# Combination by neighbouring tokens with 1 MB stores, and the softmax exponent a step later, in a long convolution with a soft mixture of experts

## Chip, cores, metric

One core of one Trainium2 chip. Times are device microseconds (us) of that core. In the profiles PE is the engine that runs this kernel's matrix products (PEld its weight loads), ACT its functions such as the exponent, DVE and POOL (GpSimd) its vector work, and SP issues nearly all of its DMA transfers. SBUF is where the kernel's tiles lie (those of PE's products apart), on up to 128 partitions; HBM is what the transfers read and write at the other end (146.18 MB read and 128.52 MB written in the profile of before); PE's products are written to tiles named `bank`, `ap` or `op`, from which ACT or DVE "evict" them to SBUF (0.58 us for one of 128x512 on ACT, L251 of before). The kernel before: median 1210.75 us of 3 runs (1209.6 to 1213.64).

## The reference, cut to what matters

```python
# 8 batches of 5696 tokens of 128 channels, all float32
y = irfft(rfft(x, n=2*S) * rfft(h, n=2*S))[:, :S]     # long convolution
x = y.reshape(45568, 128)
logits = x @ phi                                      # 32 slots: 8 experts of 4
d = softmax(logits, over tokens);  slot_input = d.T @ x
slot_out = relu(slot_input @ w1[e]) @ w2[e]           # per expert, hidden size 1024
c = softmax(logits, over slots)
return c @ slot_out                                   # 45568 x 128, 23.33 MB
```

`d` needs all tokens before the experts can start, so the combination `c @ slot_out` and all stores of the output come at the very end. `c` is kept transposed until then, that of the early chunks in HBM and at the end all of it in SBUF (`cT`).

## The kernel before

The convolution is done by two levels of small transforms. One loop of 95 steps runs everything in a pipeline: `stage_a` and `stage_b1/b2` ("units", up to three a step) are the transforms, `stage_c1` makes a chunk's `y`, and the stages after it the logits and both softmaxes. Every second step a new window of two chunks gets a common maximum: `window_top` and `window_row` make it (`mr`), GpSimd subtracts it (`d`), ACT takes the exponent. I call these window steps, the others plain steps. A chunk `c` is at `stage_c1` in step `c + 26`.

```python
    def stage_c3(c):                       # logits, then the softmax over slots
        ...
        nc.gpsimd.tensor_tensor(out=ct[...], in0=L[...], in1=rm..., op=AL.subtract)   # L329
        nc.scalar.activation(ct[:, :, :], ct[:, :, :], AF.Exp)                        # L332
        cs[c] = ct

    def stage_c3b(c):                      # row sums on DVE (L338-L340), product on GpSimd (L341)
    def stage_c4(c):                       # transpose c on PE (L349), evict on ACT

    # ... one step of the loop (cut)
        slot_b()                           # a unit: stage_b1(u), then stage_b2(u - 1)
        if c1 is not None: stage_c2(c1)
        if new: window_top(r // WC)
        if c is not None: stage_c1(c)
        if new: window_row(r // WC)        # mr, d = L - mr on GpSimd, exp(d) on ACT
        slot_b()
        if c1 is not None: stage_c3(c1)
        if t < NA: stage_a(t, 1); fold(t + 1, 1)
        slot_b()
        if c1 is not None: stage_c3b(c1)
        if chunk(2) is not None: stage_c4(chunk(2))

    # the end: 14 groups of rows r, all batches in one product
    sizes = [1] + [8] * 9 + [4] * 4
    for size in sizes:
        ...                                # 4 products per row, evictions on ACT and DVE
        for b in range(B):                 # a batch is 16 partitions
            k = 2 * NJ * b
            nc.sync.dma_start(out=ov[b, :, r0:r0 + size, :],
                              in_=o_[k:k + 2 * NJ, 0:size, :, :].rearrange("p r q d -> p r (q d)"))
```

What matters for the order: in the timelines of this case, DVE and ACT run their instructions in the order of this program, and one that waits holds up those behind it. In the kernel before, ACT starts L332 at 1057.71 after a wait of 2.10 us, and L354 behind it, whose product (L349) ended at 1055.55, follows only at 1058.03. DVE starts L338 at 1058.16 after a wait of 1.27 us, and L399 behind it, whose product (L397) ended at 1057.09, follows only at 1058.93.

## Time and profile before

| part of the span (from the trace) | us |
|---|---|
| start, to the first `stage_c1` product (L290, chunk 0) | 195.7 |
| loop, chunks 0 to 46 | 673.2 |
| late steps, chunks 46 to 55 (no `stage_a` any more) | 103.8 |
| drain, chunks 55 to 63 (no units any more) | 68.1 |
| last chain, chunk 63 to the last update of `acc` | 23.4 |
| experts, to the copy that makes `so4` | 15.6 |
| combination and stores, to the end | 129.9 |

The parts are cut at starts of instructions in one profiled run, so they sum to its span of 1209.6 us.

### The profile page before, as it was taken

The page shows a single profiled execution, that of the slowest core. Times are in us where ns is not written, and L with a number is a line of the kernel's source. Part 1 is how long each engine was busy: PE and PEld are TensorE (multiplying, and loading weights), DVE is VectorE, ACT ScalarE, POOL GpSimd, SP SyncE. Part 2 cuts the span into 40 slices and gives each one's busy share as a digit, 9 for nine tenths or more (in the row PEclk, how much of TensorE's full clock was granted, in tenths as well). Part 3 has the DMA queues.
Part 4 walks back from the last instruction along what each step waited for, and adds up shares of the span by engine and source line. Part 5 has one row for each costly group of instructions (what it writes and reads, how often), then busy time and mean ns, then how long its engine had stood idle before and what let it go on. Part 6 is the DMA issues. An engine that isn't in the chain of part 4 may idle for free.

```text
span 1209.6 us, 19085 instructions
## 1 busy us (share of the span) xinstructions
PE 1068.5 (88%) x6295; PEld 714.1 (59%) x6295; DVE 669.5 (55%) x1574; ACT 491.8 (41%) x1109; POOL 316.0 (26%) x352
## 2 busy tenths in 40 slices
PE   7788999999999999999999999999999989774430
PEld 3345665666666666666666666666667655453430
DVE  3144665666666666656665666666677745442210
ACT  4475444444444444444444444444433325421210
POOL 6433222233222322232222222222111114300000
PEclk9899999999999999999999999999999988877555
DMA  8999999887887788788788887887677766608888
GB/s 229 286 298 295 325 289 301 241 248 220 248 236 222 221 234 234 220 246 234 222 228 245 233 234 214 246 241 223 193 235 236 220 182 183 188 15 194 188 193 186
DMA packets 181576, 275.98 MB, mean 228 GB/s; under 512 B 14712, under 2 KB 121208, under 8 KB 175719
## 3 DMA queue, kind: packets, MB, share of 16 engines
q1 hardware_dynamic: 180903, 274.31, 79.5%
q8 instruction: 52, 0.85, 0.3%
q10 hardware_dynamic: 576, 0.46, 0.2%
q14 instruction: 45, 0.37, 0.1%
HBM read 146.18 MB, written 128.52 MB: 227 GB/s over the span
## 4 chain that ended last, share of the span: by engine, by line
PE 72%; SPq 10%; DVE 6%; DMA 5%; ACT 2%; issue 2%; POOL 2%; POOLq 0%; DVEq 0%; ACTq 0%
PE bank L182 18%; PE bank L290 17%; PE bank L248 12%; PE bank L212 12%; SPq L673 9%; PE bank L315 5%; PE bank L307 3%; DMA gt<-f 3%; PE ap L442 2%; DMA f<-fst 1%; POOL d L425 1%; DVE y L296 1%; DVE y L297 1%; DVE cm L322 1%; DVE pr L230 1%
## 5 line engine op out<-in xcount | busy, mean ns | idle before, releaser
L182 PE MATMUL bank<-x,s 128*128 128x512 f32 x576 | 279.4, 613 | 7.1 <-POOL x L171 7.1
L290 PE MATMUL bank<-zc,i 128*128 128x512 f32 x512 | 237.1, 607 | 5.3 <-DMA zc<-z 5.3
L212 PE MATMUL bank<-gt,wt 128*128 128x256 f32 x810 | 214.0, 387 | 17.0 <-DMA gt<-f 16.4
L171 POOL TENSOR_TENSOR x<-xc 89x512 f32<-89x512 f32 x144 | 182.9, 1271 | 134.9 <-PE bank L182 109.9
L212 PEld LDWEIGHTS bank<-gt,wt 128*128 128x128 f32 x810 | 151.0, 191 | 103.8 <-issue 75.9
L230 DVE TENSOR_TENSOR pr<-bank,Hr 128x512 f32<-128x512 f32 (+1 forms) x184 | 123.8, 673 | 132.4 <-PE bank L212 132.4
L248 PE MATMUL bank<-yf,vt 128*128 128x256 f32 x720 | 186.8, 381 | 9.9 <-DVE yf L236 5.0
L184 ACT ACTIVATE fst<-bank 90x512 f32<-90x512 f32 x288 | 162.1, 588 | 66.2 <-PE bank L182 54.5
L251 ACT ACTIVATE zst<-bank 128x512 f32<-128x512 f32 (+1 forms) x184 | 107.0, 582 | 178.4 <-PE bank L248 162.1
L182 PEld LDWEIGHTS bank<-x,s 128*128 128x128 f32 x576 | 102.6, 193 | 99.0 <-issue 61.9
L248 PEld LDWEIGHTS bank<-yf,vt 128*128 128x128 f32 x720 | 135.3, 190 | 36.3 <-ACT zst L251 6.5
L290 PEld LDWEIGHTS bank<-zc,i 128*128 128x128 f32 x512 | 94.3, 194 | 100.2 <-issue 96.6
L296 DVE TENSOR_TENSOR y<-bank,yo 89x512 f32<-89x512 f32 x64 | 44.0, 687 | 149.7 <-PE bank L290 82.3
L329 POOL TENSOR_TENSOR ct<-L,rm 89x256 f32<-89x256 f32 x64 | 39.2, 613 | 333.8 <-DVE rm L327 226.4
L230 DVE TENSOR_TENSOR pi<-bank,Hi 128x512 f32<-128x512 f32 (+1 forms) x184 | 122.7, 667 | 0.0
L315 PEld LDWEIGHTS bank<-phi,yt 128*89 128x89 f32 x1024 | 91.5, 160 | 15.9 <-ACT yt L308 10.9
L315 PE MATMUL bank<-phi,yt 128*89 128x32 f32 x1024 | 90.0, 242 | 8.1 <-ACT yt L308 8.1
L662 PE MATMUL op<-so,cT 32*128 32x128 f32 x712 | 43.5, 377 | 57.2 <-ACT o L670 56.8
L425 POOL TENSOR_TENSOR d<-L,mr 89x256 f32<-89x256 f32 x64 | 45.3, 727 | 167.7 <-DVE mr L417 167.7
L234 DVE TENSOR_TENSOR yf<-pr,pi 128x256 f32<-128x256 f32 (+1 forms) x184 | 80.3, 436 | 6.4
L332 ACT ACTIVATE ct<-ct 89x256 f32<-89x256 f32 x64 | 26.7, 417 | 122.7 <-POOL ct L329 122.7
L662 PEld LDWEIGHTS op<-so,cT 32*128 32x128 f32 x712 | 40.4, 272 | 60.2 <-ACT o L670 59.2
(78 smaller groups left out, 906.4 us busy)
## 6 DMA issues: line engine op xcount, KB each, us to landing
f<-fst SPq DMA_DIRECT2D x144, 360.0 KB
gt<-f SPq DMA_DIRECT2D x198, 256.0 KB
zc<-z SPq DMA_DIRECT2D x64, 720.0 KB
z<-zst SPq DMA_DIRECT2D x176, 256.0 KB
xc<-in_x_dram SPq DMA_DIRECT2D x64, 320.0 KB
out_dram<-o SPq DMA_DIRECT2D x72, 256.0 KB
c_t<-cst SPq DMA_DIRECT2D x54, 89.0 KB
cl<-c_t SPq DMA_DIRECT2D x6, 712.0 KB
```

Source lines behind the costliest of these rows:

```text
L171: nc.gpsimd.tensor_tensor(out=y_[0:R1, :, :], in0=t_[:, 0, :, :], in1=t_[:, 1, ::-1, :], op=AL.subtract if comp else AL.add)
L182: nc.tensor.matmul(p[:, :], s1[:, tab[G], :], src[:, :, :].rearrange("p n d -> p (n d)"), start=True, stop=True)
L184: nc.scalar.activation(st[:, :, G, :], p[0:N1, :].rearrange("p (n d) -> p n d", d=D), AF.Copy)
L212: nc.tensor.matmul(p[:, q * 256:(q + 1) * 256], wt[:, 2 * i + q, :], t_[:, q, :, :].rearrange("p c d -> p (c d)"), start=True, stop=True)
L230: nc.vector.tensor_tensor(out=t[:, 0:n, :, :], in0=pv[:, 0:n, :, :], in1=H[:, 2 * i:2 * i + n, :].unsqueeze(2).broadcast_to([P, n, 2, D]), ...
L234: nc.vector.tensor_tensor(out=y_[:, 0:n, 0, :], in0=pr[:, 0:n, 0, :], in1=pi[:, 0:n, 1, :], op=AL.subtract)
L248: nc.tensor.matmul(p[:, q * 256:(q + 1) * 256], vt[:, 2 * i + q, :], y_[:, q, :, :].rearrange("p c d -> p (c d)"), start=True, stop=True)
L251: nc.scalar.activation(st[:, 0:n, :], p[:, 0:n * 256].rearrange("p (q c) -> p q c", q=n), AF.Copy)
L290: nc.tensor.matmul(p[:, :], i1[:, tabs[q], :], t_[:, o, :, q, :], start=(q == 0), stop=(q == 1))
L315: nc.tensor.matmul(p[0:R1, i * NSL:(i + 1) * NSL], yt[:, i, :], phi[:, :], start=True, stop=True)
L662: nc.tensor.matmul(pq[q][:, k * D:(k + 1) * D], cT[rows, r0 + i + k, :], so4[rows, :], start=True, stop=True)
L673: nc.sync.dma_start(out=ov[b, :, r0:r0 + size, :], in_=o_[k:k + 2 * NJ, 0:size, :, :].rearrange("p r q d -> p r (q d)"))
```

## The change

The intent: stores of 1 MB from all 128 partitions, an exponent that ACT need not wait for, and w2 in longer runs. Core of the diff:

```diff
@@ the exponent leaves stage_c3 and comes a step later, after the window's row
-        nc.scalar.activation(ct[:, :, :], ct[:, :, :], AF.Exp)
         cs[c] = ct
+    def stage_c3x(c):
+        nc.scalar.activation(cs[c][:, :, :], cs[c][:, :, :], AF.Exp)
...
         if new:
             window_row(r // WC)
+        c2 = chunk(2)
+        if c2 is not None:
+            stage_c3x(c2)
+            stage_c3b(c2)
         slot_b()
...
-        if c1 is not None:
-            stage_c3b(c1)
-        if chunk(2) is not None:
-            stage_c4(chunk(2))
+        if chunk(3) is not None:
+            stage_c4(chunk(3))
@@ placement of c from HBM into cT: the mirrored half from ACT to GpSimd; 3 buffers, not 2
-        nc.scalar.activation(cT[:, :, e_ - n:e_], st[...], AF.Copy)
+        nc.gpsimd.tensor_copy(out=cT[:, b, :, e_ - n:e_], in_=st[...])
@@ combination: 8 rows of one batch per product, 4 products per store
-    ov = out.rearrange("(b r j n) d -> b j r (n d)", b=B, r=R1, n=CH)
+    ov = out.rearrange("(b t) d -> b t d", b=B)
...
+            nc.sync.dma_start(
+                out=ov[b, t0:t0 + n * RW * N2, :].rearrange("(w p n) d -> p w (n d)", p=P, n=CH),
+                in_=o_[:, 0:n, :, :].rearrange("p w q d -> p w (q d)"))
@@ w2
-                in_=moe_w2[2 * i:2 * i + 2].rearrange("e (c p) d -> p e c d", p=P))
+                in_=moe_w2[2 * i:2 * i + 2].rearrange("e (p c) d -> p e c d", p=P))
```

Cut: the hidden layer is evicted in the order that the new w2 wants; `cT` is indexed batch first; the one row left over goes out in a last store of 256 KB; `ct` has three buffers, `c4`, `dg` one, `ones` is narrower; the output tile is half as large and has five buffers, not three.

More of the change, by code (lines that the diff above doesn't have):

```diff
@@ L113 @@
     make_identity(nc, ident)
-    ones = const.tile([P, P], F32, name="ones")
+    ones = const.tile([P, R1], F32, name="ones")
     nc.gpsimd.memset(ones[:, :], 1.0)
@@ L124 @@
     ypool = work.enter_context(tc.tile_pool(name="ypool", bufs=1))
-    mid, inner = ExitStack(), ExitStack()
+    mid, inner, cload = ExitStack(), ExitStack(), ExitStack()
     ps = mid.enter_context(tc.tile_pool(name="ps", bufs=6, space=PSUM))
@@ L327, in stage_c3 @@
         nc.vector.reduce_max(out=rm[:, :], in_=L[:, :, :], axis=AX.X)
-        ct = cpool.tile([R1, 2 * CH, NSL], F32, name="ct", tag="ct")
+        ct = cpool.tile([R1, 2 * CH, NSL], F32, name="ct", tag="ct", bufs=3)
         nc.gpsimd.tensor_tensor(out=ct[:, :, :], in0=L[:, :, :],
@@ L364, in place @@
         b, j = divmod(c, NJ)
-        return tail["cT"][:, :, 2 * NJ * b + (2 * NJ - 1 - j if f else j)]
+        return tail["cT"][:, b, :, 2 * NJ - 1 - j if f else j]
     def load_c(c0, n):
@@ L374, in place_all @@
         b, j = divmod(c0, NJ)
-        k = 2 * NJ * b
+        e_ = 2 * NJ - j
         cT = tail["cT"]
-        nc.gpsimd.tensor_copy(out=cT[:, :, k + j:k + j + n],
+        nc.gpsimd.tensor_copy(out=cT[:, b, :, j:j + n],
                               in_=st[:, 0:n, 0, :].rearrange("p j r -> p r j"))
-        e_ = k + 2 * NJ - j
-        nc.scalar.activation(cT[:, :, e_ - n:e_],
-                             st[:, n - 1::-1, 1, :].rearrange("p j r -> p r j"), AF.Copy)
+        nc.gpsimd.tensor_copy(out=cT[:, b, :, e_ - n:e_],
+                              in_=st[:, n - 1::-1, 1, :].rearrange("p j r -> p r j"))
     mrows, downs, scales = {}, {}, {}
@@ L387, in window_max @@
         cm = cms[w % 2]
-        c4 = cpool.tile([R1, Q, NSL], F32, name="c4", tag="c4")
+        c4 = cpool.tile([R1, Q, NSL], F32, name="c4", tag="c4", bufs=1)
         nc.vector.tensor_tensor(out=c4[:, :, :],
@@ L406, in window_top @@
             downs[w] = df
-        dg = cpool.tile([P, NSL], F32, name="dg", tag="dg")
+        dg = cpool.tile([P, NSL], F32, name="dg", tag="dg", bufs=1)
         nc.vector.tensor_scalar(out=dg[:, :], in0=ident[:, 0:NSL], scalar1=top[:, w:w + 1],
@@ L414, in window_row @@
         p = bank()
-        nc.tensor.matmul(p[0:R1, 0:NSL], ones[:, 0:R1], dg[:, :], start=True, stop=True)
+        nc.tensor.matmul(p[0:R1, 0:NSL], ones[:, :], dg[:, :], start=True, stop=True)
         mr = cpool.tile([R1, NSL], F32, name="mr", tag="mr")
@@ L555 @@
             last = work.enter_context(tc.tile_pool(name="last", bufs=1))
-            tail["cT"] = last.tile([P, R1, B * 2 * NJ], F32, name="cT")
-            tail["pool"] = inner.enter_context(tc.tile_pool(name="cload", bufs=2))
+            tail["cT"] = last.tile([P, B, R1, 2 * NJ], F32, name="cT")
+            tail["pool"] = cload.enter_context(tc.tile_pool(name="cload", bufs=3))
             w2s = last.tile([P, E, NFC, D], F32, name="w2s")
@@ L576 @@
                 out=w2s[:, 2 * i:2 * i + 2, :, :],
-                in_=moe_w2[2 * i:2 * i + 2].rearrange("e (c p) d -> p e c d", p=P))
+                in_=moe_w2[2 * i:2 * i + 2].rearrange("e (p c) d -> p e c d", p=P))
     assert not (ys or Ls or ds or cs or prods or gs or zs or xs or folded or wait_b2
                 or kept or landed)
+    cload.close()
     rep4 = last.tile([P, Q, NSL], F32, name="rep4")
@@ L606 @@
     big = inner.enter_context(tc.tile_pool(name="big", bufs=2))
-    hid = big.tile([P, EG, F], F32, name="hid", tag="big")
+    hid = big.tile([P, EG, NFC, P], F32, name="hid", tag="big")
     hidT = big.tile([P, EG, NFC, P], F32, name="hidT", tag="big")
@@ L614 @@
                                  w1s[:, g * Q + q, f0:f0 + FH], start=True, stop=True)
+            dst = hid[:, g, :, f0 // NFC:(f0 + FH) // NFC]
+            src = p[:, :].rearrange("p (c k) -> p k c", k=NFC)
             if f0:
-                nc.vector.tensor_scalar(out=hid[:, g, f0:f0 + FH], in0=p[:, :], scalar1=0.0,
-                                        scalar2=None, op0=AL.max)
+                nc.vector.tensor_scalar(out=dst, in0=src, scalar1=0.0, scalar2=None, op0=AL.max)
             else:
-                nc.scalar.activation(hid[:, g, f0:f0 + FH], p[:, :], AF.Relu)
+                nc.scalar.activation(dst, src, AF.Relu)
     for g in range(EG):
@@ L624 @@
                 nc.tensor.transpose(p[:, k * P:(k + 1) * P],
-                                    hid[:, g, (k0 + k) * P:(k0 + k + 1) * P], ident[:, :])
+                                    hid[:, g, k0 + k, :], ident[:, :])
             (nc.vector.tensor_copy if k0 else nc.scalar.copy)(
@@ L646 @@
     cT = tail["cT"]
+    cL = last.tile([P, B, 2 * NJ], F32, name="cL")
+    nc.gpsimd.tensor_copy(out=cL[:, :, :], in_=cT[:, :, R1 - 1, :])
     ops = work.enter_context(tc.tile_pool(name="ops", bufs=8, space=PSUM))
-    opool = work.enter_context(tc.tile_pool(name="opool", bufs=3))
-    ov = out.rearrange("(b r j n) d -> b j r (n d)", b=B, r=R1, n=CH)
-    RG, G4 = 8, 4
-    sizes = [1] + [RG] * 9 + [G4] * 4
-    assert sum(sizes) == R1
-    r0 = 0
-    for size in sizes:
-        o_ = opool.tile([P, RG, Q, D], F32, name="o", tag="o")
-        for i in range(0, size, G4):
-            n = min(G4, size - i)
+    opool = work.enter_context(tc.tile_pool(name="opool", bufs=5))
+    ov = out.rearrange("(b t) d -> b t d", b=B)
+    RW = P // (2 * NJ)
+    NV = R1 // RW
+    assert NV * RW == R1 - 1
+    G4 = 4
+    for b in range(B):
+        for w0 in range(0, NV, G4):
+            n = min(G4, NV - w0)
+            lone = b == B - 1 and w0 + G4 >= NV
+            o_ = opool.tile([P, G4, Q, D], F32, name="o", tag="o")
             pq = [ops.tile([P, 512], F32, name="op", tag="op") for _ in range(Q)]
-            for k in range(n):
+            for k in range(n + lone):
                 for q in range(Q):
                     rows = slice(q * NSL, (q + 1) * NSL)
-                    nc.tensor.matmul(pq[q][:, k * D:(k + 1) * D], cT[rows, r0 + i + k, :],
+                    r0 = (w0 + k) * RW
+                    nc.tensor.matmul(pq[q][:, k * D:(k + 1) * D],
+                                     cT[rows, b, r0:r0 + RW, :] if k < n else cL[rows, :, :],
                                      so4[rows, :], start=True, stop=True)
             for q in range(Q):
-                dst = o_[:, i:i + n, q, :]
-                src = pq[q][:, 0:n * D].rearrange("p (k d) -> p k d", d=D)
+                dst = o_[:, 0:n + lone, q, :]
+                src = pq[q][:, 0:(n + lone) * D].rearrange("p (k d) -> p k d", d=D)
                 if q % 2:
@@ L670 @@
                     nc.scalar.activation(dst, src, AF.Copy)
-        for b in range(B):
-            k = 2 * NJ * b
-            nc.sync.dma_start(out=ov[b, :, r0:r0 + size, :],
-                              in_=o_[k:k + 2 * NJ, 0:size, :, :].rearrange("p r q d -> p r (q d)"))
-        r0 += size
+            t0 = w0 * RW * N2
+            nc.sync.dma_start(
+                out=ov[b, t0:t0 + n * RW * N2, :].rearrange("(w p n) d -> p w (n d)", p=P, n=CH),
+                in_=o_[:, 0:n, :, :].rearrange("p w q d -> p w (q d)"))
+            if lone:
+                nc.sync.dma_start(
+                    out=ov[:, NV * RW * N2:, :].rearrange("b (j n) d -> b j (n d)", n=CH),
+                    in_=o_[:, n, :, :].rearrange("p q d -> p (q d)"))
     work.close()
```

## The prediction

> **What bounds the kernel now.** I first read the page's 40 slices, to see which stages there are. One slice is 30.2 us.
>
> ```profile
> PE   7788999999999999999999999999999989774430
> DVE  3144665666666666656665666666677745442210
> ACT  4475444444444444444444444444433325421210
> PEclk9899999999999999999999999999999988877555
> DMA  8999999887887788788788887887677766608888
> GB/s 229 286 298 295 325 289 301 241 248 220 248 236 222 221 234 234 220 246 234 222 228 245 233 234 214 246 241 223 193 235 236 220 182 183 188 15 194 188 193 186
> ```
>
> PE is full in slices 5 to 32. Then comes a drain in which nobody is full, one slice without DMA (the expert MLP), and four slices in which only DMA works, at a flat 190 GB/s. Stretches of the trace give the borders (PE, PEld, DVE, ACT, POOL busy; then clock, DMA share, GB/s):
>
> ```profile
> 300.00:600.00 300.00, 300.00 (x1669) 201.39 (x1668) 189.91 (x448) 130.46 (x294) 90.49 (x103) 1.00 0.81 234
> 600.00:900.00 300.00, 299.18 (x1710) 202.44 (x1710) 193.53 (x460) 127.45 (x290) 82.90 (x97) 1.00 0.79 228
> 983.00:1062.00 79.00, 63.71 (x465) 39.70 (x463) 38.70 (x99) 32.49 (x82) 27.80 (x36) 0.82 0.63 183
> 1062.00:1082.00 20.00, 16.53 (x277) 10.34 (x281) 6.83 (x20) 4.09 (x11) 0.24 (x1) 0.75 0.01 2
> 1100.00:1194.00 94.00, 32.84 (x448) 30.59 (x448) 19.30 (x31) 16.28 (x32) 0.00 (x0) 0.57 0.88 192
> ```
>
> So there are three regimes: a loop bound by PE (whatever delays PE there is lost for good, whatever else gets shorter is worth nothing), a drain from about 973 to 1062 bound by chains of latency, and stores from 1080 to 1209.6 bound by DMA. The change touches all three.
>
> Because the loop is full, I then read a step of it by the timeline, filtered by eye to what the exponent will meet. This is a step with a new window (every second one, when `mr` and `d` are made):
>
> ```profile
> 680.83 0.27 PE L415 MATMUL bank<-dg,ones 128*89 128x32 f32 x2
> ...
> 682.31 0.18 DVE L417 COPY mr<-bank 89x32 f32<-89x32 f32 x1
> 682.41 0.68 DVE L230 TENSOR_TENSOR pr<-bank,Hr 128x512 f32<-128x512 f32 x1
> 682.57 1.42 POOL L425 TENSOR_TENSOR d<-L,mr 89x256 f32<-89x256 f32 x2 [6.05 <-DVE mr L417]
> ...
> 684.01 0.42 ACT L428 ACTIVATE d<-d 89x256 f32<-89x256 f32 x1 [0.27 <-POOL d L425]
> 684.19 0.41 DVE L236 TENSOR_TENSOR yf<-pr,pi 128x256 f32<-128x256 f32 x1
> 684.34 0.57 ACT L251 ACTIVATE zst<-bank 128x512 f32<-128x512 f32 x1
> ...
> 686.63 1.03 PE L248 MATMUL bank<-yf,vt 128*128 128x256 f32 x4
> ```
>
> The reader is to see that DVE has `yf` ready at 684.60 and PE takes it at 686.63: 2.03 us of slack, no more.
>
> [...] The trace of before agrees: each of its stores reads 16 partitions, and in the DMA packet records after 1082 us the 2 KB packets pile up at 84, 150 and 300 ns, mean 147.7[...]; elsewhere in the same trace a 2 KB packet mostly takes 84. [...] The trace agrees: at 1057.71 ACT starts L332 after 2.10 us of waiting for GpSimd, and the evictions behind it (L354) come only after that.
>
> **Part 1, the stores.** Before, the last product operand (`so4`) is ready at 1080.05 and the end is 1209.6: 129.5 us for 23.33 MB in 112 stores of 256 KB or less. After: 24 stores of 1 MB or 768 KB from 128 partitions, plus one of 256 KB. Products and evictions keep number and size (712 products, 128x512 evictions of 0.52 us on ACT and 0.62 on DVE): two per engine and megabyte, 1.24 us, against about 3 us for its DMA, so they stay hidden, at half clock too. The packets stay 2 KB and 11392. If nearly all take 84 to 90 ns, 16 engines give 364 to 390 GB/s when always busy; before reaches 326 GB/s over 120 to 150 us with mostly 1 KB packets, at a share of 1.00. I take 355 GB/s: 65.7 us. To that come about 2 us for the first products and evictions and 4 us for the first store's start and the last one's landing: 71.5 us in place of 129.5. **Gain 58 us** (330 GB/s gives 53, 380 gives 62).
>
> **Part 2, the exponent in the loop.** The order of instructions in the changed build shows where it goes: right after `mr`, DVE now has the three `rs` instructions, ahead of `pr`, `pi`, `yf` of the unit; and they need the exponent, which on ACT stands behind both exponents of `d`, which need GpSimd's two subtractions. In a window step that is a new detour: DVE waits from 682.5 until the exponent ends. ACT: second `d` exponent 684.01, then the exponent from 684.34 to 684.76; then `rs`, 0.77 us (as at 989.46, from the first one's start to the start of what follows at 990.23), so `pr` starts at about 685.57 where it was 682.41. `yf` comes 3.16 us later, at 687.76; with 0.15 us to PE, L248 starts at 687.9 and not 686.63. **PE loses 1.28 us per window step**, and as it is full elsewhere it wins nothing back. Windows fall in every odd step from 29 on; 22 of them (29 to 71) have this form: 28 us. In steps 73 to 79 the first transform is over and PE comes for `yf` at once (910.41, `yf` at 910.10): about 3.0 us each, of which 0.54 that PE waited for the next `yf` anyway are saved: 4 x 2.5 = 10 us. In plain steps the exponent is long done when DVE gets there, `rs` costs 0.8 us of a slack of 2, so nothing; where the slack is gone (steps 72, 74, 76, 78, 80) 0.5 to 0.8 each: 3 us. **Loss 41 us.** What it saves in the loop is ACT's wait for GpSimd (93.4 us over 49 steps from 300 to 983), worth nothing: PE did not wait for it.
>
> **Part 3, the drain.** There the same move pays. L290 starts of the last nine chunks stand 8.5 us apart (972.7 to 1040.8, 68.1 us), on a loop through L319, DVE, GpSimd, the exponent, L354, the placement L380 (1.39 us, 7 of them), L308 and L315. The change takes the exponent's wait and L380 out of ACT's line (placement goes to GpSimd, 2.8 us a step, which it has). PE's own work is 7.05 us a step: 8 x 7.05 = 56.4, plus some 3 us for the third `zc` (memset, then load; the wait was 2.94), plus 3 us of half clock after it: 62.4, gain 6. The last chain (1040.8 to 1064.1) loses L380 and the `rs` triple ahead of the maximum, about 7 us, but the last transposition now waits for the late exponent, 3 us back: gain 4. **Gain 10 to 11 us.**
>
> **Part 4, the rest.** w2 in 4 KB runs: its four loads issue from 1039 and are in place well before L632 starts at 1075.12 without a wait: hidden, 0. The hidden layer's evictions read PSUM with a stride of 8; four of 0.60 to 0.69 us behind 5.78 us of products: at worst 0.5. Buffers (`ct` 3, `c4` and `dg` 1) are a step apart: 0.
>
> **Sum:** 1210.75 - 58 + 41 - 11 = 1182.8, say 1183.
>
> **Rivals.** (a) The loop does not lose, since the detour is absorbed in slack that I mis-see: then about 1142. For it: GpSimd and ACT are 30 to 45% busy. Against it: the timeline's 2.03 us are exact and DVE runs in order. (b) The stores stay slow, because writing HBM and not reading SBUF is the limit: at 192 GB/s for good, 1240; at 270 GB/s, 1204. For it: no stretch of before has stores alone from 128 partitions. Against it: 84 ns is the commonest packet even there[...]. (c) The late exponent stalls PE more, say 2.5 us per window, through banks or folds behind it: 1210. For it: GpSimd's subtraction and fold come about 2.5 us later too; against it: their next use is a step away.
>
> **Range and chances.** The terms are uncertain by about 6 (stores), 9 (loop) and 5 (drain), so 12 in all; with the rivals I widen it to 1163 to 1204. 2% faster is below 1186.5, just beside my middle: 0.57 faster, 0.40 same, 0.03 slower.
>
> **What would show it.** Stores at 340 to 370 GB/s with 2 KB packets near 84 ns; window steps of 16.4 us beside plain ones of 15.1 between 300 and 870, with PE waiting at L248 for `yf` some 26 times and DVE waiting for `ct` before `rs`; L290 steps of 7 to 7.5 us in the drain. A loop that ends as early as before, or stores under 300 GB/s, would make it wrong.

That stores from 128 partitions would bring packets of 84 to 90 ns is the author's estimate, from the trace of before: its stores from 16 partitions have 46% of their 2 KB packets at 80 to 95 ns, where before 1080 us 74% of the 2 KB packets lie there, most often at 84. The 2 and 4 us beside it are estimates too; in the same trace the first store is issued 1.4 us after `so4`, its first packet comes 0.8 us later, and the end comes 4.3 us after the last store's issue. The 3 us of half clock in Part 3 are the 6.43 us that L290 took at 991.22, after the wait of 2.94, where it takes 3.67 at 981.61 (granted clock 0.50 from 990.0 to 996.8 us). That DVE runs in order is shown above, with L338 and L399.

## More of the kernel before

Beside the views that the prediction shows, two answers of the wait view of the kernel before are needed for comparison (for 300 to 983 us; columns: total, times, longest):

```profile
DVE rs L338 <- ACT ct L332: 8.8, 7, 1.3
PE bank L248 <- DVE yf L236: 3.1, 8, 0.5
```

PE hardly ever waits for `yf` in the loop, and DVE hardly ever for the exponent.

## The result, and the profile after

The changed kernel takes 1191.64 us (median of 4; 1190.54 to 1192.09), against 1211.79 for the kernel before in 4 runs. The ratio is 0.9833, 95% interval 0.9813 to 0.9853. Ratios here are the mean time of one kernel's runs over that of the other's of the same rounds, so not quite the ratio of the medians.

The small net hides large terms:

| part | before | after | after minus before | predicted |
|---|---|---|---|---|
| start | 195.7 | 201.4 | +5.7 | 0 |
| loop, chunks 0 to 46 | 673.2 | 700.3 | +27.1 | +28 |
| late steps, 46 to 55 | 103.8 | 121.9 | +18.1 | +13 |
| drain, 55 to 63 | 68.1 | 60.9 | -7.2 | -6 |
| last chain | 23.4 | 21.7 | -1.7 | -4 |
| experts | 15.6 | 14.8 | -0.8 | 0 |
| combination and stores | 129.9 | 68.8 | -61.1 | -58 |

The slices of the page, to be held against those of before (a slice is now 29.7 us; a digit is the busy share of the slice in tenths, for PEclk the granted clock in tenths):

```profile
PE   7697999999999999999999999999998888897783
PEclk9899999999999999999999999999999999999855
DMA  7999998877787787778776877777765665584199
GB/s 212 292 276 298 287 319 270 279 235 230 215 237 220 212 239 219 217 202 238 225 223 199 243 225 223 215 228 226 225 199 176 196 202 176 170 253 182 68 379 341
```

The four slices of 190 GB/s at the end have become two of 379 and 341. Stretches of the trace (same columns as before) give the loop and the stores:

```profile
300.00:600.00 300.00, 289.82 (x1593) 191.97 (x1592) 184.84 (x429) 127.65 (x280) 86.24 (x97) 1.00 0.78 224
600.00:900.00 300.00, 290.17 (x1616) 192.78 (x1614) 186.57 (x437) 128.30 (x281) 84.91 (x97) 1.00 0.74 216
1125.00:1180.00 55.00, 42.91 (x622) 39.80 (x619) 26.47 (x45) 22.07 (x44) 0.00 (x0) 0.63 1.03 379
```

PE was busy 300.00 of 300 us in the loop and is now 289.82: ten microseconds in each 300 are gone. The waits from 300 to 983 us name them:

```profile
DVE rs L340 <- ACT ct L335: 53.9, 23, 2.4
PE bank L248 <- DVE yf L236: 30.2, 28, 2.7
```

A window step by the timeline shows how one leads to the other:

```profile
706.39 0.18 DVE L418 COPY mr<-bank 89x32 f32<-89x32 f32 x1
706.64 1.41 POOL L426 TENSOR_TENSOR d<-L,mr 89x256 f32<-89x256 f32 x2 [6.05 <-DVE mr L418]
...
708.09 0.42 ACT L429 ACTIVATE d<-d 89x256 f32<-89x256 f32 x1 [0.27 <-POOL d L426]
708.41 0.40 ACT L335 ACTIVATE ct<-ct 89x256 f32<-89x256 f32 x1
...
708.91 0.42 DVE L340 TENSOR_REDUCE rs<-ct 89x8 f32<-89x256 f32 x1 [2.35 <-ACT ct L335]
...
709.68 0.64 DVE L230 TENSOR_TENSOR pr<-bank,Hr 128x512 f32<-128x512 f32 x1
...
711.29 0.42 DVE L236 TENSOR_TENSOR yf<-pr,pi 128x256 f32<-128x256 f32 x1
...
711.86 1.10 PE L248 MATMUL bank<-yf,vt 128*128 128x256 f32 x4 [0.98 <-DVE yf L236]
```

After `mr`, DVE stands 2.35 us for the exponent, which stands on ACT behind two exponents of `d`, which stand behind GpSimd. `pr` starts 3.29 us after `mr` and no longer 0.10. PE comes for `yf` and waits. Window steps take 16.3 us and plain ones 15.0, where both took 15.0 to 15.1.

### The profile page after: what moved, and what is told of

Read it like the earlier page. It is cut to its first block, busy times and chain, and to the rows that moved or that the text cites. A ratio compares the mean times of both kernels' runs of the same rounds, so it can differ in the third digit from the quotient of the medians.

```text
span 1189.9 us, 18952 instructions
## 1 busy us (share of the span) xinstructions
PE 1081.8 (91%) x6295; PEld 717.1 (60%) x6295; DVE 682.0 (57%) x1576; ACT 492.7 (41%) x1105; POOL 324.9 (27%) x360
## 5 line engine op out<-in xcount | busy, mean ns | idle before, releaser
L182 PE MATMUL bank<-x,s 128*128 128x512 f32 x576 | 282.6, 619 | 7.0 <-POOL x L171 7.0
L290 PE MATMUL bank<-zc,i 128*128 128x512 f32 x512 | 234.3, 600 | 2.6 <-DMA zc<-z 2.6
L212 PE MATMUL bank<-gt,wt 128*128 128x256 f32 x810 | 216.8, 391 | 18.3 <-DMA gt<-f 15.5
L248 PE MATMUL bank<-yf,vt 128*128 128x256 f32 x720 | 192.2, 389 | 42.8 <-DVE yf L236 38.7
L184 ACT ACTIVATE fst<-bank 90x512 f32<-90x512 f32 x288 | 167.3, 592 | 104.7 <-PE bank L182 91.9
L290 PEld LDWEIGHTS bank<-zc,i 128*128 128x128 f32 x512 | 93.0, 192 | 95.8 <-issue 94.5
L343 POOL TENSOR_TENSOR ct<-ct,rs 89x256 f32<-89x256 f32 x64 | 39.3, 614 | 261.8 <-DVE rs L342 259.2
L234 DVE TENSOR_TENSOR yf<-pr,pi 128x256 f32<-128x256 f32 (+1 forms) x184 | 92.6, 503 | 6.3
L236 DVE TENSOR_TENSOR yf<-pr,pi 128x256 f32<-128x256 f32 (+1 forms) x184 | 75.6, 411 | 0.0
L429 ACT ACTIVATE d<-d 89x256 f32<-89x256 f32 x64 | 26.7, 417 | 108.5 <-POOL d L426 108.5
```

The source lines that it names most:

```text
L182: nc.tensor.matmul(p[:, :], s1[:, tab[G], :], src[:, :, :].rearrange("p n d -> p (n d)"), start=True, stop=True)
L184: nc.scalar.activation(st[:, :, G, :], p[0:N1, :].rearrange("p (n d) -> p n d", d=D), AF.Copy)
L212: nc.tensor.matmul(p[:, q * 256:(q + 1) * 256], wt[:, 2 * i + q, :], t_[:, q, :, :].rearrange("p c d -> p (c d)"), start=True, stop=True)
L234: nc.vector.tensor_tensor(out=y_[:, 0:n, 0, :], in0=pr[:, 0:n, 0, :], in1=pi[:, 0:n, 1, :], op=AL.subtract)
L236: nc.vector.tensor_tensor(out=y_[:, 0:n, 1, :], in0=pr[:, 0:n, 1, :], in1=pi[:, 0:n, 0, :], op=AL.add)
L248: nc.tensor.matmul(p[:, q * 256:(q + 1) * 256], vt[:, 2 * i + q, :], y_[:, q, :, :].rearrange("p c d -> p (c d)"), start=True, stop=True)
```

## The experiments

Nine kernels ran, one of them (e4) twice, all with correct results. "Before" is the kernel before on the same chip (medians 1209.2 to 1210.4).

### The exponent back in its old place, the rest as changed (e1)

```diff
             stage_c3(c1)
+            stage_c3x(c1)
...
-        c2 = chunk(2)
-        if c2 is not None:
-            stage_c3x(c2)
-            stage_c3b(c2)
...
+        if c1 is not None:
+            stage_c3b(c1)
-        if chunk(3) is not None:
-            stage_c4(chunk(3))
+        if chunk(2) is not None:
+            stage_c4(chunk(2))
```

> The changed kernel with the exponent, its row sums and its transposition back at their old places of a step; stores, w2 and placement on GpSimd as changed. Theory (DVE stands behind the late exponent in every window step and PE has no slack for it): window steps go from 16.3 back to 15.1 us, the 45 us that the loop lost (27 up to chunk 46, 18 up to chunk 55) come back and some 8 us of the drain are lost again: 1191.6 - 45 + 8 = about 1155 us (1147 to 1160). Rival (the loop lost its time to something else in the change, for example to the smaller buffers or the new transfers): stays at 1185 to 1195, window steps still 16.3 us.

Measured: 1155.66 us (1153.24 to 1158.8), ratio 0.9542 (0.9504 to 0.958). Loop 673.2 and late steps 103.8 us, to the tenth as before, window steps 15.1; drain 70.7, last chain 23.8, stores 68.8. Without the moved exponent the change is worth 4.6%. The rival that something else in the change harms the loop falls.

### The exponent moved alone, in the kernel before (e2)

The reverse: the kernel before with the first part of the diff, and the buffer sizes that let it fit.

> The kernel before with the moved exponent alone (with the buffer sizes that it needs: ct 3, c4 and dg 1, the smaller ones). Theory: the same loss without the gain of the stores: 1211 + 45, less some 3 to 7 us of the drain (the placement on ACT stays, so less than in the changed kernel) = 1246 to 1255 us; stores still at about 190 GB/s. Rival (the exponent's move is harmless or good by itself, the loop's loss came with something else): 1203 to 1211 us.

Measured: 1250.9 us (1249.34 to 1252.4), ratio 1.0323 (1.0279 to 1.0367). Its two waits from 300 to 983 us are the changed kernel's:

```profile
DVE rs L340 <- ACT ct L335: 53.9, 23, 2.3
PE bank L248 <- DVE yf L236: 30.2, 28, 2.7
```

Loop 700.2, late steps 124.6, drain 60.6, last chain 21.7, stores 127.6. So the exponent's move costs 3% of the whole by itself, though it shortens the drain by 7.5 us.

### Row sums later, exponent where the change has it (e3)

```diff
         if c2 is not None:
             stage_c3x(c2)
-            stage_c3b(c2)
         slot_b()
...
         slot_b()
+        if c2 is not None:
+            stage_c3b(c2)
         if chunk(3) is not None:
```

> The changed kernel; the exponent stays on ACT where it is, behind both exponents of d, but the row sums on DVE and the product on GpSimd come after the step's third unit. Theory (what costs is that DVE stands behind the exponent): window steps 15.1 us, the drain as short as in the changed kernel: 1191.6 - 45 = about 1147 us (1142 to 1153). Rival (ACT itself, an exponent behind GpSimd's subtractions and ahead of the evictions, is what PE waits for): window steps stay at 16.3 us, 1185 to 1192 us.

Measured: 1149.63 us (1148.14 to 1151.61), ratio 0.9492 (0.9458 to 0.9526). Loop 673.0, late steps 104.9. ACT's exponent still stands behind GpSimd's subtractions here, and PE loses nothing in the loop (and 1.1 us in the late steps): it is DVE's standing behind it that costs, not ACT's. Drain (62.6) and last chain (23.0) are 1.7 and 1.3 us longer than in the changed kernel, so the early row sums had been good for something there.

### Exponent ahead of the window's two, row sums right after `mr` (e4)

```diff
             stage_c1(c)
-        if new:
-            window_row(r // WC)
         c2 = chunk(2)
         if c2 is not None:
             stage_c3x(c2)
+        if new:
+            window_row(r // WC)
+        if c2 is not None:
             stage_c3b(c2)
```

> The changed kernel with the exponent ahead of the window's two exponents of d on ACT; row sums on DVE right after mr as changed. Theory (the wait costs, not the place of the row sums): DVE finds the exponent done, the row sums' 0.8 us fit into 2.03 us of slack in the 22 early windows (15.1 us steps), and cost 0.3 to 0.8 us in the four late ones: 1147 to 1153 us. Rival (the three row sum instructions ahead of the unit's products cost by themselves): window steps of 15.5 to 16 us, 1165 to 1185 us.

Measured: 1142.28 us (1141.29 to 1144.7), ratio 0.9433 (0.9399 to 0.9468), better than the range. Timeline of a window step:

```profile
681.55 0.41 ACT L335 ACTIVATE ct<-ct 89x256 f32<-89x256 f32 x1
...
684.00 0.18 DVE L418 COPY mr<-bank 89x32 f32<-89x32 f32 x1
684.10 0.41 DVE L340 TENSOR_REDUCE rs<-ct 89x8 f32<-89x256 f32 x1
...
686.77 0.42 DVE L236 TENSOR_TENSOR yf<-pr,pi 128x256 f32<-128x256 f32 x1
...
688.32 1.03 PE L248 MATMUL bank<-yf,vt 128*128 128x256 f32 x4
```

DVE goes from `mr` straight to the row sums; `yf` is ready at 687.19, 1.13 us before PE takes it. The loop is 673.0 us again, with the row sums in the same place on DVE as in the changed kernel: the wait cost, not the work. What my range missed is the end: drain 58.4 and last chain 19.0, because the exponents no longer stand behind a window's `d` (last chain 2.7 us less than in the changed kernel, 1.8 of them after the last `mr`). The late steps, at 107.7, pay about 4 us for the row sums ahead of `pr`, where there is no slack.

### Stores of 16 partitions (s1), stores of 128 partitions but 256 KB (s2)

```diff
-            nc.sync.dma_start(out=<1 MB, 128 partitions>, in_=o_[:, 0:n, :, :]...)
+            for p0 in range(0, P, 16):                    # s1
+                nc.sync.dma_start(out=ovw[p0:p0 + 16, :, :], in_=o_[p0:p0 + 16, 0:n, :, :]...)
+            for k in range(n):                            # s2
+                nc.sync.dma_start(out=ovw[:, k, :], in_=o_[:, k, :, :]...)
```

> The changed kernel with each store of 1 MB cut into eight of 16 partitions each (same places in HBM, same 2 KB packets). Theory[...]: packets near 150 ns in the mean again with heaps at 84, 150 and 300, about 190 GB/s, the part after so4 grows from 69 to about 127 us: 1245 to 1253 us. Rival (writing with 128 partitions helps by the order of addresses in HBM, or by nothing that the partitions do): 1191 to 1200 us.

> The changed kernel with each store cut into its windows: 88 stores of 256 KB, each from all 128 partitions. 256 KB is the size that the kernel before had. Theory (partitions, not size): packets stay at 84 to 95 ns, 320 to 350 GB/s, 1190 to 1197 us. Rival (fewer and larger stores are what pays, a fixed cost per store): the part after so4 goes back to 100 us or more, 1220 us or more.

Measured: s1 1244.62 us (1242.14 to 1245.18), ratio 1.0277 (1.0246 to 1.0308), stores 122.9 us. s2 1192.73 us (1190.57 to 1196.92), ratio 0.9856 (0.9819 to 0.9893), stores 71.0 us. The stretches of the store part, s1 first, then s2 (last two columns: DMA share, GB/s):

```profile
1170.00:1230.00 60.00, 23.68 (x271) 21.03 (x268) 12.14 (x21) 10.23 (x20) 0.00 (x0) 0.50 0.88 203
```

```profile
1125.00:1175.00 50.00, 42.92 (x620) 39.24 (x620) 24.87 (x42) 20.84 (x42) 0.00 (x0) 0.67 0.95 358
```

The 11392 packets of 2 KB, the same in all four kernels:

| | mean ns | share at 80 to 95 | at 140 to 170 | at 280 to 320 |
|---|---|---|---|---|
| before | 147.7 | 46% | 24% | 12% |
| s1 | 141.7 | 49% | 16% | 9% |
| after | 89.2 | 94% | under 1% | under 1% |
| s2 | 86.6 | 91% | under 1% | 0 |

With the addresses in HBM and the packets unchanged, cutting by partitions alone brings the old rate and the old heaps back; cutting by size alone does almost nothing (2.2 us). It is the 128 partitions (stores 122.9 us from 16 at a time, 71.0 and 68.8 from 128), and not the 1 MB. (The stores of s1 are also smaller, 128 and 96 KB; but before ran at the same rate with 256 KB from 16 partitions, and s2 at the high one with 256 KB.) Nor is SP's issuing the limit: the DMA engines are busy for a share of 0.88 in s1, and the packets themselves take longer. Why the packets from 16 partitions take longer (141.7 ns in s1, 89.2 after) was not shown.

### w2 as before (w1)

e4 with the 512 B runs of w2 and the hidden layer in its old order.

```diff
-                in_=moe_w2[2 * i:2 * i + 2].rearrange("e (p c) d -> p e c d", p=P))
+                in_=moe_w2[2 * i:2 * i + 2].rearrange("e (c p) d -> p e c d", p=P))
-            dst = hid[:, g, :, f0 // NFC:(f0 + FH) // NFC]
-            src = p[:, :].rearrange("p (c k) -> p k c", k=NFC)
+            dst = hid[:, g, f0:f0 + FH]
+            src = p[:, :]
```

> The version with the exponent first (e4, 1142.3 us), with w2 in 512 B runs and the hidden layer in its old order, as in the kernel before. Theory (w2 lands long before it is needed, the strided evictions are hidden): the same within 2 us, 1140.5 to 1144.5, and the part from the last update of acc to so4 the same within 0.5 us. Rival (512 B runs hold up the last loads of z and c or the MLP): 1146 us or more.

Measured: 1142.98 us (1140.99 to 1144.18), ratio 0.9436 (0.9402 to 0.9469), against 0.9433 of e4: no difference. The experts' part is 15.6 us against 14.9. That is 0.7, a little over the 0.5 that I allowed, but this part read 14.9 and 15.1 in two runs of e4 and 14.8 to 16.4 in kernels with the same code there, so it says nothing. The transfer is hidden.

### Half of the placement back on ACT (p1)

e4 with the mirrored copy on ACT, as before.

```diff
-        nc.gpsimd.tensor_copy(out=cT[:, b, :, e_ - n:e_], in_=st[...])
+        nc.scalar.activation(cT[:, b, :, e_ - n:e_], st[...], AF.Copy)
```

> The version with the exponent first (e4), with the mirrored half of the placement back on ACT as before. In e4 a DVE maximum of 128x1 takes 3.03 us where GpSimd makes both copies of the placement, against some 0.16 otherwise: it stands until they end. Theory A (the drain is bound by PE's own 7 us a step and this wait is beside it): the maximum then takes about 1.8 us at most, the drain stays at 58.4 us and the last chain at 19 within 1.5 us, 1141 to 1145 us. Theory B (the wait is on the path): 1137 to 1140 us. Theory C (ACT's 1.39 us are on the path, as they were before): drain and last chain together 3 to 8 us longer, 1145 to 1150 us.

Measured: 1143.63 us (1143.28 to 1146.08), ratio 0.9451 (0.9422 to 0.9479). The wait in question is best seen in the changed kernel's drain, where `top` is one number per partition:

```profile
1056.54 0.61 POOL L329 TENSOR_TENSOR ct<-L,rm 89x256 f32<-89x256 f32 x1 [0.62 <-DVE rm L327]
1056.81 3.03 DVE L402 TENSOR_TENSOR top<-top 128x1 f32<-128x1 f32 x1
1057.10 1.40 POOL L379 COPY cT<-cl 128x712 f32<-128x712 f32 x1
...
1058.44 1.38 POOL L381 COPY cT<-cl 128x712 f32<-128x712 f32 x1
```

In p1 the same instruction takes 1.73 us, with one copy on GpSimd. L405, of the same shape, takes 0.16 (at 1059.88). In both kernels L402 ends 0.02 us after the last copy (1059.84 and 1059.82 here, 1013.78 and 1013.76 in p1), so I take it that the copies hold it. But the drain is 59.5 (58.4 in e4) and the last chain 18.9 (19.0): theory A, the wait lies beside PE's own 7 us a step. Moving the copy to GpSimd was neither gain nor loss once the exponent stood well. (A small gain and a small loss that cancel would look the same: the drain read 57.7 to 59.0 us in e4, e4 again and w1.)

### Both good places together (e5, with e4 again for comparison)

```diff
+        late = bool(us)
-        if c2 is not None:
+        if c2 is not None and not late:
             stage_c3b(c2)
         slot_b()
...
         slot_b()
+        if c2 is not None and late:
+            stage_c3b(c2)
```

> The version with the exponent first (e4); where a step has units of the first transform left, the row sums on DVE come after the third unit (as in e3), and right after mr in the drain (as in e4). Theory (in the late steps with no slack even 0.8 us of row sums ahead of pr delay PE; in the drain the early row sums shorten the last chain): the stretch from chunk 46 to 55 as in e3 (104.9 us instead of 107.7), drain and last chain as in e4 (58.4 and 19.0): 2 to 3 us under e4 in the same call. Rival (the two places interact, the late ones push work into the drain): no gain, or slower than e4.

> The same kernel as e4, for comparison with e5 on one chip: 1141 to 1144 us, stretch from chunk 46 to 55 of 107.7 us, drain 58.4, last chain 19.0.

Measured, 5 runs each on one chip: e5 1139.94 us (1136.75 to 1140.46), ratio 0.9411 (0.9388 to 0.9435); e4 again 1145.2 us (1143.13 to 1145.55), ratio 0.9459 (0.9434 to 0.9484). The medians are 5.3 us apart, more than expected: late steps 103.7 us, as before, against 109.4 in this run of e4, drain 57.4 against 57.7, last chain 19.0 in both. In e5 PE's loop is full again:

```profile
300.00:600.00 300.00, 300.00 (x1672) 201.82 (x1671) 190.70 (x450) 134.21 (x293) 89.93 (x102) 1.00 0.81 233
600.00:900.00 300.00, 299.24 (x1697) 202.81 (x1696) 193.35 (x458) 131.21 (x289) 83.51 (x97) 1.00 0.78 227
```

This version beats the kernel before by 5.9% and the changed one by about 4%.

## Why the prediction was right, point by point

The time (1183 predicted, 1191.64 measured) lies in the range of 1163 to 1204, and the outcome, just short of 2%, was given 0.40 beside 0.57 for the other side of the line, so the side that it held likelier did not come. In the profiled runs the miss is what is left of terms that in part cancel: late steps +5.1, last chain +2.3 and start +5.7 against stores -3.1 and drain, loop and experts together -2.9. The terms, by its own steps:

- **Stores, gain 58:** right, 61.1. The assumed 84 to 90 ns per packet was 89.2, and the assumed 355 GB/s was 379 in the middle. s1 and s2 show the 128 partitions as the cause (stores 122.9 us against 71.0), and rival (b), HBM as the limit at 192 to 270 GB/s, fell.
- **Exponent in the loop, 28 for 22 windows:** right, 27.1, and 1.22 us in a typical window (16.34 against 15.12). `yf` late by 3.2 us against 2.03 of slack was read from before alone. e1, e2, e3 and e4 each confirm a part of the chain. Rival (a), absorbed by slack, would have been 1142; that is about what e4 gives, where the slack does suffice. Rival (c), 2.5 us per window, fell in the loop.
- **Late steps, 13:** the mis-sized term, 18.1. The plain ones came as said (0.6 to 0.8 us each, 3.2 in all). Of the four windows one lost 2.3 us, near the 2.5 that I said, and three 3.6 to 4.9. In all four PE waits for `yf`, 2.70 to 3.07 us; behind three of these waits products run at half speed for 3.4 to 6.8 us, and in the window that lost 2.3 us they do not. The first window and, last line, that one:

```profile
922.18 2.04 PE L248 MATMUL bank<-yf,vt 128*128 128x256 f32 x4 [2.70 <-DVE yf L236]
...
925.47 2.07 PE L212 MATMUL bank<-gt,wt 128*128 128x256 f32 x4
...
980.88 1.10 PE L248 MATMUL bank<-yf,vt 128*128 128x256 f32 x4 [2.71 <-DVE yf L236]
```

  Both groups take 1.03 to 1.13 us when PE has not waited. The clock records of the profile agree: the granted clock is 0.50 from 921.1 to 927.9, from 951.8 to 955.2 and from 1009.8 to 1013.3 us, and 1.00 from 976 to 985. The first drop, at 921.1, is 1.6 us into the wait of 2.70. In e2 there is half clock after all four waits, and each window loses 3.7 to 5.2 us. I had counted the wait and not the slow time after it. Why the clock fell after one wait of 2.70 us and not after another of 2.71 stays open.
- **Drain and last chain, gain 6 and 4:** 7.2 and 1.7. The last chain is the second mis-sized term. What the late exponent gives back was as counted: from the last `mr` to the last update of `acc` 6.70 us against 3.57, so 3.1. The saving ahead of `mr` was not: 14.99 against 19.79, so 4.8 in place of about 7. One part of the mechanism is not borne out: I had counted on the copy L380 leaving ACT. e2, with that copy still on ACT, has the same drain and last chain as the changed kernel (60.6 and 21.7), and e1, with the copy moved and the exponent back, has no gain (70.7 and 23.8, before 68.1 and 23.4); the gain is that of the exponent, the row sums and the transposition, which e2 moves together.
- **w2 and buffers, 0:** right (w1 for w2; for the buffers e1, whose loop is that of before).
- **What was not in the sum:** the start took 5.7 us longer in the profiled run, before any moved instruction runs. s1 and s2, with the same code there, show 196.2 and 199.2 against 201.4, so this is scatter between runs (195.7 to 201.4 over twelve traces), but it is part of the profiled difference. What causes the scatter stays open.

## What to carry to other kernels

On an engine that runs its instructions in the order of the program, as DVE and ACT did here (L340 stood 2.35 us for the exponent and `pr` behind it started 3.29 us after `mr`, no longer 0.10), "a step later" is not a safe place by itself: ask what the moved instruction stands behind there, and what stands behind its consumer, and compare the delay with the slack of the engine that is full; here 3.2 us against 2.03 cost 3% of the kernel, and the same instruction ahead of the window's exponents cost nothing in the loop. When a change with a large sure gain comes out small, cut the trace at the same instructions in both kernels and compare part by part before arguing. For stores at the end of a kernel, try first to spread each over all 128 partitions: here that took the stores from 122.9 us (s1) to 71.0 (s2), and the size, 256 KB or 1 MB, mattered far less (71.0 to 68.8).
